# Batch by batch through two sweeps: reordering the first blocks of a fused attention and MoE kernel

## The chip, the cores and the metric

The kernel runs on one core of a Trainium2 chip. The metric is the device time of one execution in microseconds (us); the smaller, the better. Five engines work from queues of their own, each in the order in which the program was written: PE (TensorE: matmuls and transposes; its weight loads are listed as PEld), DVE (VectorE), ACT (ScalarE), POOL (GpSimd) and SP (SyncE), which issues DMA transfers. An engine whose next instruction has to wait holds back all that stands behind it.

## The reference

For 8 batches of 8 heads, 576 rows of 64 numbers, and a feature map phi of 32 columns:

```
a = softmax(phi, axis=2)                    # phi: batch, head, 576 rows, 32 columns
k_m = einsum('bhsm,bhsd->bhmd', a, k);  v_m = einsum('bhsm,bhsd->bhmd', a, v)
attn = softmax(q @ k_m.T / 8)               # 576 x 32
x = concat_heads(attn @ v_m)                # 4608 x 512
x = (h - tanh(h)) @ w_out,  h = x @ w_in    # 512 -> 2048 -> 512
out = elu(x @ w_in2) @ w_out2               # 512 -> 2048 -> 512
```

The first softmax runs along the axis of 576 rows, and its sums have 32 entries for each head. The inputs are float32 or float64 (the weights); products are formed from a high and a low part (hi, lo), three matmuls for each product.

## The kernel before

**Units.** A unit of attention is one batch and four heads; there are 16. `unit` (L108) is a generator: between two `yield`s it writes a few instructions. One call of `units.round()` (L253) advances every live unit by one such piece. A unit finds the column maxima of phi (`cmax`, DVE, L120), subtracts them (L135), takes the exponential `a` (ACT, L140), sums it over the rows (`asum`, DVE, L143), multiplies `a` with k and v on PE (`km`, L150; the sums' last step is L153), divides (L159 to L165), transposes, forms the scores (L195), takes the second softmax (L200 to L208) and stores its hi and lo parts in DRAM (`p_dram`, L222). Two Attention objects with buffers of their own, at0 and at1, take the units: 0 and 2 run in at0, all others in at1; units 0 and 1 start at rounds 0 and 1, units 2 and 3 at rounds 8 and 9, unit u from 4 on at round 22 + 7(u-4).

**Blocks.** Layer 1 works in 64 blocks, each one half of a batch (288 tokens, number n) in one of four sweeps `sw` (512 of the 2048 hidden columns). A block is two steps. A step computes `h_ps` (PE, L331, 12 matmuls) out of `p` and `vw`, then h - tanh(h) on ACT, POOL and DVE (`g_a` to `g_d`, L336 to L365), and beside it the output products `x_ps` (L376) of an earlier block, copied to `x2` tiles and stored (L391). The product v_m w_in (`vw`, L316) is formed in halves, four for each group of four blocks, in the fourth block of the group before. At L614 the blocks are listed: a group is a sweep and a pair of batches, so the first four blocks are two batches in sweep 0 and the next four are the same two batches in sweep 1.

**Weights.** `conv` (L524) loads 512 KB of float64 weights (`raw`), splits them on ACT, DVE and POOL (L48 to L60) and leaves hi and lo parts. `cv.round()` advances these generators; `need` calls it until a given part is there. Layer 2's weights go to DRAM the same way during layer 1. After block 63 layer 2 runs (L669), and the change doesn't touch it.

Of the kernel before, what the change touches and what calls it, by code (L numbers as in the profile page):

```python
# [8 lines left out]
F32 = mybir.dt.float32  # L9
# [53 lines left out]
class Attention:  # L63
# [5 lines left out]
    def __init__(self, tc, ctx, const, ins, vm, p_dram, side, psum):  # L69
        nc = tc.nc  # L70
        self.nc, self.ins, self.vm, self.p_dram = nc, ins, vm, p_dram
        self.ident, self.pmask, self.ones = const["ident"], const["pmask"], const["ones"]
        pool = lambda name, n: ctx.enter_context(
            tc.tile_pool(name=name + side, bufs=n, side=side, reuse_waits="tile"))
        self.wk = pool("at_wk", 1)
        self.sm = pool("at_sm", 2)
        self.sc_p = pool("at_sc", 2 if side == "left" else 1)
        self.ps = psum
        self.q_p = pool("at_q", 2)
        self.loaded = {}  # L80
# [4 lines left out]
        self.asum = fix.tile([128, 4, M], F32, name="asum")  # L85
        for t in (self.a, self.asum, self.kv):
            nc.gpsimd.memset(t[96:], 0.0)
        nc.gpsimd.memset(self.kT, 0.0)

    def load(self, u, what):  # L90
# [9 lines left out]
        elif what == "phi":  # L100
            t = self.wk.tile([96, 4, 6, M], F32, tag="phi", name="phi")
            nc.sync.dma_start(out=t, in_=view("phi", 0, 4))
        else:
            t = self.q_p.tile([96, 2, 6, D], F32, tag="q", name="q")
            nc.sync.dma_start(out=t, in_=view("q", 0 if what == "q0" else 2, 2))
        self.loaded[u, what] = t

    def unit(self, u, nxt, eng, first_p=None):  # L108
# [5 lines left out]
        kv, a, kT, asum = self.kv, self.a, self.kT, self.asum  # L114
# [5 lines left out]
        nc.vector.tensor_reduce(cmax, ph.rearrange("p h c m -> p h m c"), axis=AX.X, op=ALU.max)  # L120
# [22 lines left out]
        nc.vector.tensor_reduce(asum[:96], a[:96].rearrange("p c h m -> p h m c"), axis=AX.X, op=ALU.add)  # L143
        yield
# [12 lines left out]
        rm = sm.tile([128, 2, 1], F32, tag="rm", name="rm")  # L157
# [3 lines left out]
        nc.vector.tensor_scalar(rm[:, :, 0], self.pmask, rs, None, op0=ALU.mult)  # L161
# [3 lines left out]
        nc.vector.tensor_tensor(vbd, twice(1), rm.to_broadcast([128, 2, D]), op=ALU.mult)  # L165
        yield
        s = self.sc_p.tile([128, 18, M], F32, tag="s", name="s")
        for pr in range(2):
            qt = self.loaded.pop((u, f"q{pr}"))
            qT = wk.tile([128, 2, 3, 96], F32, tag="qT", name="qT")  # L170
            for h in range(2):
# [7 lines left out]
                yield  # L179
# [37 lines left out]
        yield  # L217
        for c, t in enumerate(first_p or ()):
# [64 lines left out]
class Moe1:  # L283


    def __init__(self, tc, ctx, const, p_dram, x2_dram):
# [7 lines left out]
        self.vw_p = pool("vw", 1)  # L294
        self.vw, self.p, self.g, self.x2, self.work, self.x2_pool = {}, {}, {}, {}, {}, {}
# [10 lines left out]
    def vw_half(self, vm, wi, pg, po, pars=(0, 1)):  # L306
        nc = self.nc
        if po == 0:
            for par in pars:
                self.vw[par, pg] = [self.vw_p.tile([128, 2, 256], F32R, tag=f"vw{pg % 2}_{par}{t}", name="vw")  # L310
# [180 lines left out]
def moe_kernel(tc, q, k, v, phi, w1, w2, w3, w4, out):  # L491
    nc = tc.nc
    with ExitStack() as top, tc.manual_schedule():
# [84 lines left out]
        def unit(u):  # L578
            if u % 4 == 0 and u:
                new_vm(u // 4)  # L580
            if u in (0, 2):
                yield from at0.unit(u, 2 if u == 0 else 2 * B, nc.vector if u == 0 else nc.gpsimd,
                                    first_p if u == 0 else None)
            else:
                yield from at1.unit(u, 3 if u == 1 else u + 1, nc.vector if u < 2 else nc.gpsimd,
                                    first_p if u == 1 else None)
# [7 lines left out]
        while 1 not in p_done:  # L594
            units.round()
# [19 lines left out]
        blocks = [(ss, bp, sub, j) for ss, bp, sub in groups for j in range(4)]  # L615
# [67 lines left out]
        for bi, (ss, bp, sub, j) in enumerate(blocks):  # L683
# [17 lines left out]
            vw_next = None  # L701
            if bi == 1:
                vw_next = (0, 0, (1,))
            elif j == 3 and nxt:
                vw_next = (nbp, 2 * nxt[0], (0, 1))
            if at0_open and 2 in p_done:
# [21 lines left out]
            for i in range(2):  # L728
# [92 lines left out]
```

## Time and profile before

| what | value |
|---|---|
| median of 3 runs | 1772.01 us (1768.45 to 1779.19) |
| the profiled execution's own time | 1771.73 us |
| its span, first to last instruction | 1770.0 us |
| PE busy | 1618.5 us, 91% of the span |
| DVE, ACT, POOL busy | 1225.3, 954.7, 766.3 us |
| chain that ended last | PE 70%, DMA 10%, DVE 7%, ACT 5% of the span |

A busy PE is no proof of a PE at its peak: at the lower of its two clocks the same matmul takes twice as long and is counted as busy all the same. The shares are means over stages with different limits, so the rows further down are taken by stage.

### The profile page before, as it was taken

The numbers are of one execution on the slowest core, as the hardware profiler recorded it, in microseconds if no ns is written. First come the engines' busy times: TensorE is split into PE (matmuls) and PEld (weight loads), VectorE is DVE, ScalarE is ACT, GpSimd is POOL, SyncE is SP. The second block draws the span as 40 slices with busy tenths as digits, with TensorE's granted clock in tenths as the row PEclk, the third lists the DMA queues.
The fourth block names the chain that finished last, engine by engine and source line by source line (L and its number), as shares of the span: only waits on it lengthen the run. The fifth ranks groups of instructions, "written<-read, shape, count | busy, mean of one in ns | idle before, by whom it ended". The sixth has DMA issues, their size and how long they took to land.

```text
span 1770.0 us, 30078 instructions
## 1 busy us (share of the span) xinstructions
PE 1618.5 (91%) x11496; PEld 1494.5 (84%) x11496; DVE 1225.3 (69%) x1805; ACT 954.7 (54%) x1713; POOL 766.3 (43%) x539
## 2 busy tenths in 40 slices
PE   4546887987998999999989999999999999999998
PEld 3446777877898999999989999999999999999997
DVE  5768876778899988888854555555555555555554
ACT  2445675766888888888864333333333333333332
POOL 2144554636676666666653222222222222222222
PEclk9668999999999999999999999999999999999999
DMA  9546557567566455666567521212222121111110
GB/s 226 157 121 181 146 158 201 169 191 221 187 225 195 160 177 212 217 215 223 189 191 291 195 61 60 60 60 60 60 60 59 54 58 56 57 60 57 58 36 25
DMA packets 140935, 238.40 MB, mean 135 GB/s; under 512 B 8184, under 2 KB 102392, under 8 KB 138744
## 3 DMA queue, kind: packets, MB, share of 16 engines
q1 hardware_dynamic: 140792, 236.49, 43.0%
q8 instruction: 91, 1.49, 0.4%
q14 instruction: 52, 0.43, 0.1%
HBM read 159.78 MB, written 75.50 MB: 133 GB/s over the span
## 4 chain that ended last, share of the span: by engine, by line
PE 70%; DMA 10%; DVE 7%; ACT 5%; issue 3%; POOL 2%; SPq 1%; DVEq 0%; POOLq 0%; ACTq 0%
PE h_ps L432 23%; PE o_ps L469 22%; PE x_ps L376 14%; PE h_ps L331 8%; DMA x_dram<-x 5%; DMA raw<-in_moe_w_in_dram 3%; PE vw_ps L316 2%; DVE s L356 1%; DVE vw L321 1%; DMA kv<-in_v_dram 1%; ACT t L342 1%; DMA xr<-x_dram 1%; DMA phi<-in_phi_dram 1%; ACT u L343 1%; ACT big L345 1%
## 5 line engine op out<-in xcount | busy, mean ns | idle before, releaser
L376 PE MATMUL x_ps<-g,w 128*128 128x288 f32 x3072 | 454.5, 301 | 30.4 <-DVE vw L321 9.6
L376 PEld LDWEIGHTS x_ps<-g,w 128*128 128x128 f32 x3072 | 427.2, 192 | 41.6 <-ACT x L383 11.0
L458 POOL TENSOR_TENSOR e<-hm,e 128x512 fp32r<-128x512 f32 x144 | 186.8, 1297 | 588.1 <-ACT e L457 435.4
L432 PEld LDWEIGHTS h_ps<-x,wi 128*128 128x128 f32 x3456 | 429.7, 190 | 11.7
L432 PE MATMUL h_ps<-x,wi 128*128 128x256 f32 x3456 | 433.2, 281 | 0.0
L469 PE MATMUL o_ps<-wo,e 128*128 128x512 f32 x1728 | 423.8, 394 | 0.7 <-POOL e L458 0.7
L469 PEld LDWEIGHTS o_ps<-wo,e 128*128 128x128 f32 x1728 | 314.8, 188 | 65.0 <-POOL e L458 1.1
L443 ACT ACTIVATE t_ps<-hm 128x512 f32<-128x512 f32 x144 | 86.7, 602 | 515.1 <-DVE hm L442 515.1
L350 POOL TENSOR_TENSOR v<-t,u 128x576 f32<-128x576 f32 x128 | 183.9, 1436 | 230.8 <-ACT u L343 208.4
L331 PE MATMUL h_ps<-p,vw 128*128 128x288 f32 x1536 | 241.8, 309 | 17.8 <-DVE s L357 6.1
L331 PEld LDWEIGHTS h_ps<-p,vw 128*128 128x128 f32 x1536 | 222.9, 199 | 20.9 <-issue 12.7
L364 POOL TENSOR_TENSOR g<-s,g 128x576 fp32r<-128x576 f32 x128 | 203.2, 1588 | 83.9 <-ACT g L363 81.3
L449 DVE SCALAR_TENSOR_TENSOR hm<-hm,t_ps 128x512 f32<-128x512 f32 x144 | 99.1, 688 | 200.6 <-ACT hm L444 200.6
L442 DVE TENSOR_SCALAR hm<-h_ps 128x512 f32<-128x512 f32 x144 | 99.6, 692 | 139.9 <-PE h_ps L432 139.9
L351 DVE TENSOR_TENSOR h_ps<-h_ps,t 128x576 f32<-128x576 f32 x128 | 97.9, 765 | 56.8 <-ACT u L343 55.6
L342 ACT ACTIVATE t<-h_ps 128x576 f32<-128x576 f32 x128 | 83.2, 650 | 82.2 <-PE h_ps L331 39.6
L356 DVE SCALAR_TENSOR_TENSOR s<-s,v 128x576 f32<-128x576 f32 x128 | 121.5, 949 | 1.8 <-POOL v L350 1.8
L321 DVE TENSOR_TENSOR vw<-vw_ps,vw 64x512 fp32r<-64x512 f32 x128 | 88.1, 688 | 40.4 <-ACT vw L319 38.4
L357 DVE COPY_PREDICATED s<-big,h_ps 128x576 f32<-128x576 uint32 x128 | 106.3, 831 | 11.3 <-DVE s L356 0.5
L345 ACT ACTIVATE big<-u,bias 128x576 f32<-128x576 f32 x128 | 97.5, 762 | 13.5 <-DVE s L357 13.5
L451 DVE TENSOR_TENSOR hm<-hm,h_ps 128x512 f32<-128x512 f32 x144 | 98.9, 687 | 5.0
L450 DVE SCALAR_TENSOR_TENSOR hm<-hm,t_ps 128x512 f32<-128x512 f32 x144 | 98.9, 687 | 4.9
(86 smaller groups left out, 1764.6 us busy)
## 6 DMA issues: line engine op xcount, KB each, us to landing
x_dram<-x SPq DMA_DIRECT2D x128, 288.0 KB
xr<-x_dram SPq DMA_DIRECT2D x72, 512.0 KB
p<-p_dram SPq DMA_DIRECT2D x62, 576.0 KB
raw<-in_moe_w_in_dram SPq DMA_DIRECT2D x32, 512.0 KB
raw<-in_moe_w_out_dram SPq DMA_DIRECT2D x32, 512.0 KB
w_dram<-wst SPq DMA_DIRECT2D x32, 512.0 KB
kv<-in_k_dram SPq DMA_DIRECT2D x16, 576.0 KB
kv<-in_v_dram SPq DMA_DIRECT2D x16, 576.0 KB
```

The costliest lines, as they stand in the source:

```text
L321: nc.vector.tensor_tensor(lo, src, r32(hi), op=ALU.subtract)
L331: nc.tensor.matmul(ps[:, j, :NB], lhsT=vw[a][:, kc, 128 * j:128 * j + 128], rhs=p[:, kc, b, :], start=(k == 0), stop=(k == 5))
L342: nc.scalar.activation(t, w[0], ACTF.Tanh)
L345: nc.scalar.activation(big, u, ACTF.Relu, bias=bias[:, 1:2])
L350: nc.gpsimd.tensor_tensor(v, t, u, op=ALU.mult)
L356: nc.vector.scalar_tensor_tensor(s, s, G_B, v, op0=ALU.add, op1=ALU.mult)
L357: nc.vector.copy_predicated(s, big.bitcast(U32), d)
L364: nc.gpsimd.tensor_tensor(g[:, 1], s, r32(g[:, 0]), op=ALU.subtract)
L376: nc.tensor.matmul(ps, lhsT=wo[pg][:, a, j, 128 * dm:128 * dm + 128], rhs=g[:, b, j, :], start=(k == 0), stop=(k == 11))
L432: nc.tensor.matmul(ps[:, j], lhsT=w3[:, a, kc, 128 * j:128 * j + 128], rhs=x[:, b, kc, :], start=(k == 0), stop=(k == 11))
L458: nc.gpsimd.tensor_tensor(e[:, 1], hm, r32(e[:, 0]), op=ALU.subtract)
L469: nc.tensor.matmul(self.acc[n][tg], lhsT=e[:, a, j, 128 * tg:128 * tg + 128], rhs=w4[:, b, j, :], start=(pg == 0 and j == 0 and i == 0), s ...
```

## The change

Layer 1's first eight blocks are put in another order: the first batch in sweep 0 and then in sweep 1, then the second batch. at0 takes unit 0 alone; at1 takes all others in a row, unit u from 2 on at round 8 + 7(u-2). The `vw` of these blocks are formed for one batch at a time, with a free slot given by `vw_first`. The sums of `a` are formed on PE out of `a` itself (six matmuls) in place of `asum` on DVE and four matmuls; the column maxima come from three elementwise steps in place of one reduction; `rm` goes and its factor is folded into `vbd`. phi is issued on ACT's queue from unit 2 on; kv and q loads are written one piece later. From block 26 on, the four halves of `vw` are spread over the last two blocks of a group, one for each step. The pool of `x2` tiles grows from 3 to 4, that of the `s` tiles (`gw`) shrinks from 3 to 2.

```diff
@@ Attention.load, unit
-            nc.sync.dma_start(out=t, in_=view("phi", 0, 4))
+            (nc.sync if u < 2 else nc.scalar).dma_start(out=t, in_=view("phi", 0, 4))
-        nc.vector.tensor_reduce(cmax, ph.rearrange("p h c m -> p h m c"), axis=AX.X, op=ALU.max)
+        nc.vector.tensor_tensor(top, ph[:, :, 0:3], ph[:, :, 3:6], op=ALU.max)
+        nc.vector.tensor_tensor(cmax, top[:, :, 0], top[:, :, 1], op=ALU.max)
+        nc.vector.tensor_tensor(cmax, cmax, top[:, :, 2], op=ALU.max)
-        nc.vector.tensor_reduce(asum[:96], a[:96].rearrange("p c h m -> p h m c"), axis=AX.X, op=ALU.add)
-        yield
-        for h in range(4):
-            nc.tensor.matmul(km[32 * h:32 * h + 32, 2 * D:], lhsT=asum[:, h], rhs=self.ones[:, :2],
-                             start=True, stop=True)
-        self.load(nxt, "kv")
+        for c in range(6):
+            nc.tensor.matmul(km[:, 2 * D:], lhsT=a[:, c].rearrange("p h m -> p (h m)"), rhs=self.ones[:, :2],
+                             start=(c == 0), stop=(c == 5))
-        nc.vector.tensor_scalar(rm[:, :, 0], self.pmask, rs, None, op0=ALU.mult)
-        nc.vector.tensor_tensor(vbd, twice(1), rm.to_broadcast([128, 2, D]), op=ALU.mult)
+        for j in range(2):
+            nc.vector.tensor_scalar(vbd[:, j], kmv[:, 1], rs, self.pmask[:, j:j + 1], op0=ALU.mult, op1=ALU.mult)
+        yield
+        self.load(nxt, "kv")
@@ Moe1.__init__
-        self.x_p = pool("x2", 3)
+        self.x_p = pool("x2", 4)
-        self.gw, self.gw1 = pool("gw", 3), pool("gw1", 1)
+        self.gw, self.gw1 = pool("gw", 2), pool("gw1", 1)
@@ moe_kernel, units and blocks
-            if u in (0, 2):
-                yield from at0.unit(u, 2 if u == 0 else 2 * B, nc.vector if u == 0 else nc.gpsimd,
-                                    first_p if u == 0 else None)
+            if u == 0:
+                yield from at0.unit(u, 2 * B, nc.vector, first_p)
-        for u, t in ((0, 0), (1, 1), (2, 8), (3, 9)):
-            units.at(t, unit(u))
-        for u in range(4, 2 * B):
-            units.at(22 + 7 * (u - 4), unit(u))
+        for u in range(2 * B):
+            units.at(u if u < 2 else 8 + 7 * (u - 2), unit(u))
-        blocks = [(ss, bp, sub, j) for ss, bp, sub in groups for j in range(4)]
+        blocks = [(0, 0, sub, j) for j0 in (0, 2) for sub in range(2) for j in (j0, j0 + 1)]
+        blocks += [(ss, bp, sub, j) for ss, bp, sub in groups[2:] for j in range(4)]
+        vw_first = {1: (0, 2, (0,), 1), 3: (0, 0, (1,), 0), 5: (0, 2, (1,), 1)}
+            if j >= 2 and bi >= 26:
+                if bi // 4 + 1 < len(groups):
+                    nss, nbp, nsub = groups[bi // 4 + 1]
+                    vw_spread = (nbp, 2 * (2 * nss + nsub) + j - 2)
+            elif bi in vw_first:
+                vw_next = vw_first[bi]
-            if at0_open and 2 in p_done:
+            if at0_open:
...
+                if vw_spread:
+                    vbp, vpg = vw_spread
+                    need("i", vpg)
+                    m1.vw_half(vm[vbp], wi[vpg], vpg, i)
```

Where the rows now stand is told by the program's order on each engine. On DVE, while the first two batches' attention runs and before the first block. Before (`asum`, `rm` and two units' divisions):

```order
L143 TENSOR_REDUCE asum<-a 96x128
L50 TENSOR_SCALAR cv_m<-cv_m 128x512
L51 TENSOR_SCALAR cv_m<-cv_m 128x512
L200 TENSOR_REDUCE smax<-s 128x18
L201 TENSOR_TENSOR s<-s,smax 128x576
L159 TENSOR_SCALAR rs<-km 128x1
L160 RECIPROCAL rs<-rs 128x1
L161 TENSOR_SCALAR rm<-pmask,rs 128x2
L163 TENSOR_SCALAR kk<-km,rs 128x128
L165 TENSOR_TENSOR vbd<-km,rm 128x128
L143 TENSOR_REDUCE asum<-a 96x128
```

The same place in the changed program:

```order
L199 TENSOR_REDUCE smax<-s 128x18
L200 TENSOR_TENSOR s<-s,smax 128x576
L157 TENSOR_SCALAR rs<-km 128x1
L158 RECIPROCAL rs<-rs 128x1
L160 TENSOR_SCALAR kk<-km,rs 128x128
L163 TENSOR_SCALAR vbd<-km,rs,pmask 128x64 x2
L50 TENSOR_SCALAR cv_m<-cv_m 128x512
```

The reductions of `a` and `rm` are gone, and unit 3's division no longer stands ahead of the first block; it follows in block 0.

On PE, around the second block's first step. Before (w_376 is part 0 of w_in, here with the second batch; w_616 and w_752 are parts of w_out):

```order
L331 MATMUL h_ps<-p,vw 128x288 x12
L150 MATMUL km<-kv,a 32x128 x24
L153 MATMUL km<-ones,asum 32x2 x4
L316 MATMUL vw_ps<-w_376,vm 128x256 x6
L376 MATMUL x_ps<-g,w_616 128x288 x6
L376 MATMUL x_ps<-g,w_752 128x288 x6
L174 MATMUL pq<-ident,q 128x96 x3
L316 MATMUL vw_ps<-w_376,vm 128x256 x6
L331 MATMUL h_ps<-p,vw 128x288 x12
```

The same place in the changed program (w_862 is part 2 of w_in, which stood two blocks later):

```order
L335 MATMUL h_ps<-p,vw 128x288 x12
L181 MATMUL kT_ps<-ident,kk 128x128
L182 MATMUL kT_ps<-ident,vbd 128x128
L320 MATMUL vw_ps<-w_862,vm 128x256 x6
L380 MATMUL x_ps<-g,w_576 128x288 x6
L380 MATMUL x_ps<-g,w_770 128x288 x6
L194 MATMUL sc<-qT,kT 64x288 x2
L127 MATMUL mT<-ident,cmax 128x96
L320 MATMUL vw_ps<-w_862,vm 128x256 x6
L335 MATMUL h_ps<-p,vw 128x288 x12
```

Parts 2 and 3 of w_in are now due in block 1, and not in block 3; w_out's parts 2 and 3 move up likewise. From the tenth block on, both programs hold the same number of units and conversions at the same block.

On PE, at a change of groups in the second half of layer 1. Before:

```order
L316 MATMUL vw_ps<-w_5814,vm 128x256 x6
L331 MATMUL h_ps<-p,vw 128x288 x12
L376 MATMUL x_ps<-g,w_6927 128x288 x6
L376 MATMUL x_ps<-g,w_7216 128x288 x6
L316 MATMUL vw_ps<-w_5972,vm 128x256 x6
L376 MATMUL x_ps<-g,w_6927 128x288 x6
L376 MATMUL x_ps<-g,w_7216 128x288 x6
L316 MATMUL vw_ps<-w_5972,vm 128x256 x6
L331 MATMUL h_ps<-p,vw 128x288 x12
```

The changed program:

```order
L320 MATMUL vw_ps<-w_5889,vm 128x256 x6
L335 MATMUL h_ps<-p,vw 128x288 x12
L380 MATMUL x_ps<-g,w_7002 128x288 x6
L380 MATMUL x_ps<-g,w_7306 128x288 x6
L380 MATMUL x_ps<-g,w_7002 128x288 x6
L380 MATMUL x_ps<-g,w_7306 128x288 x6
L320 MATMUL vw_ps<-w_6058,vm 128x256 x6
L335 MATMUL h_ps<-p,vw 128x288 x12
```

A step held two halves of `vw` with a product `x_ps` between them, and now holds one, right ahead of the next step.

## Rows read from the trace of the kernel before

**Rows 1.** Stages: us, busy PE, PEld, DVE, ACT, POOL; clock, DMA share, GB/s.

```profile
0.00:77.00 77.00, 35.70 (x332) 24.31 (x332) 54.34 (x105) 25.01 (x55) 18.84 (x22) 0.88 0.90 215
77.00:177.00 100.00, 62.47 (x424) 53.50 (x425) 72.50 (x107) 51.83 (x97) 42.64 (x30) 0.76 0.50 138
177.00:260.00 83.00, 70.96 (x638) 65.05 (x638) 67.07 (x104) 59.47 (x118) 45.54 (x32) 0.97 0.54 158
260.00:490.00 230.00, 195.81 (x1663) 179.35 (x1662) 173.75 (x271) 160.13 (x315) 125.86 (x86) 0.95 0.62 189
490.00:600.00 110.00, 102.26 (x747) 100.63 (x746) 102.72 (x152) 93.96 (x164) 73.86 (x53) 0.97 0.60 201
600.00:893.00 293.00, 286.24 (x2143) 283.58 (x2143) 259.02 (x384) 252.56 (x440) 202.58 (x140) 1.00 0.58 201
893.00:946.00 53.00, 46.05 (x317) 45.64 (x316) 30.52 (x42) 31.10 (x52) 28.56 (x19) 0.90 0.77 231
946.00:1770.00 824.00, 819.01 (x5245) 742.50 (x5244) 465.43 (x645) 280.64 (x475) 228.43 (x162) 1.00 0.22 71
```

**Rows 2.** Timeline of PE: start, us, instructions; first steps of blocks 0, 4, 9.

```profile
77.00 1.30 PE L331 MATMUL h_ps<-p,vw 128*128 128x288 f32 x4 [3.44 <-DMA p<-phl]
...
177.11 1.16 PE L331 MATMUL h_ps<-p,vw 128*128 128x288 f32 x4
...
259.54 1.86 PE L331 MATMUL h_ps<-p,vw 128*128 128x288 f32 x12
```

**Rows 3.** Stage view, the stretch from 30 to 70 us.

```profile
30.00:70.00 40.00, 20.21 (x179) 12.20 (x180) 36.33 (x65) 15.84 (x37) 10.41 (x7) 0.82 0.82 200
```

**Rows 4.** Waits from 77 to 177 us: total, times, longest.

```profile
ACT cv_m L48 <- DMA raw<-in_moe_w_in_dram: 12.3, 3, 8.2
...
PE h_ps L331 <- DMA p<-p_dram: 3.8, 1, 3.8
```

**Rows 5.** Waits from 260 to 490 us.

```profile
ACT x L383 <- DMA x_dram<-x: 28.3, 9, 5.8
```

**Rows 6.** Chain that ended last, one group of four blocks.

```profile
637.33 1.61 PE h_ps L331 x12
...
679.30 0.71 PE vw_ps L316 x6
680.01 1.61 PE h_ps L331 x12
```

**Rows 7.** Timeline of PE at a change of groups.

```profile
677.47 1.83 PE L376 MATMUL x_ps<-g,w 128*128 128x288 f32 x12 [0.91 <-DVE vw L321]
...
679.85 1.77 PE L331 MATMUL h_ps<-p,vw 128*128 128x288 f32 x12
...
684.65 1.77 PE L331 MATMUL h_ps<-p,vw 128*128 128x288 f32 x12
```

**Rows 8.** Timeline of DVE at the end of layer 1.

```profile
928.82 0.46 DVE L385 COPY x<-x_ps 128x288 f32<-128x288 f32 x1 [7.49 <-DMA x_dram<-x]
```

**Rows 9.** Groups of DVE's instructions up to 260 us: busy us, mean ns.

```profile
L120 DVE TENSOR_REDUCE cmax<-phi 96x128 f32<-96x768 f32 x10 | 15.5, 1547 | 6.1 <-DMA phi<-in_phi_dram 6.1
L143 DVE TENSOR_REDUCE asum<-a 96x128 f32<-96x768 f32 x9 | 13.6, 1506 | 1.9 <-ACT a L140 1.9
...
L161 DVE TENSOR_SCALAR rm<-pmask,rs 128x2 f32<-128x2 f32 x9 | 6.4, 710 | 0.3
```

**Rows 10.** Line 201: shortest, median, longest ns; first and last start.

```profile
L201 DVE TENSOR_TENSOR s<-s,smax x16: 757/759/1877, 46.1 to 477.3; 128x576 f32<-128x576 f32 x16
```

**Rows 11.** Timeline of SP: start and us of an issue.

```profile
120.58 4.31 SPq L530 DMA_DIRECT2D raw<-in_moe_w_in_dram  x1
...
142.05 0.32 SPq L102 DMA_DIRECT2D phi<-in_phi_dram  x1
```

**Rows 12.** Timeline of all engines within a group of four blocks.

```profile
648.49 1.76 POOL L364 TENSOR_TENSOR g<-s,g 128x576 fp32r<-128x576 f32 x1 [1.42 <-ACT g L363]
...
649.85 0.78 ACT L344 ACTIVATE s<-u,bias 128x576 f32<-128x576 f32 x1
```

More of the change, by code (lines that the diff above doesn't have):

```diff
@@ L84, in __init__ @@
         self.kT = fix.tile([128, 4, 2, M], F32, name="kT")
-        self.asum = fix.tile([128, 4, M], F32, name="asum")
-        for t in (self.a, self.asum, self.kv):
+        for t in (self.a, self.kv):
             nc.gpsimd.memset(t[96:], 0.0)
@@ L113, in unit @@
         ident = self.ident
-        kv, a, kT, asum = self.kv, self.a, self.kT, self.asum
+        kv, a, kT = self.kv, self.a, self.kT
         ps_tile = lambda shape, name: self.ps.tile(shape, F32, tag="m", name=name)
@@ L309, in vw_half @@
             for par in pars:
-                self.vw[par, pg] = [self.vw_p.tile([128, 2, 256], F32R, tag=f"vw{pg % 2}_{par}{t}", name="vw")
+                at = par if slot is None else slot
+                pool = self.vw2_p if self.vw2_p and par and pg // 2 % 2 else self.vw_p
+                self.vw[par, pg] = [pool.tile([128, 2, 256], F32R, tag=f"vw{pg % 2}_{at}{t}", name="vw")
                                     for t in range(2)]
@@ L580, in unit @@
                 new_vm(u // 4)
-            if u in (0, 2):
-                yield from at0.unit(u, 2 if u == 0 else 2 * B, nc.vector if u == 0 else nc.gpsimd,
-                                    first_p if u == 0 else None)
-            else:
-                yield from at1.unit(u, 3 if u == 1 else u + 1, nc.vector if u < 2 else nc.gpsimd,
-                                    first_p if u == 1 else None)
+            if u == 0:
+                yield from at0.unit(u, 2 * B, nc.vector, first_p)
+            else:
+                yield from at1.unit(u, u + 1, nc.vector if u < 2 else nc.gpsimd, first_p if u == 1 else None)
         first_p = [m1.new_p(0, n) for n in range(2)]
         units = Staged()
-        for u, t in ((0, 0), (1, 1), (2, 8), (3, 9)):
-            units.at(t, unit(u))
-        for u in range(4, 2 * B):
-            units.at(22 + 7 * (u - 4), unit(u))
+        for u in range(2 * B):
+            units.at(u if u < 2 else 8 + 7 * (u - 2), unit(u))
         while 1 not in p_done:
+            if units.rounds >= 7:
+                cv.half()
             units.round()
@@ L746, in moe_kernel @@
                 if vw_next:
-                    vbp, vpg, pars = vw_next
+                    vbp, vpg, pars, slot = vw_next
                     need("i", vpg + i)
-                    while ss == 0 and not all(u in vm_done for u in range(4 * vbp + 4)):
+                    while ss == 0 and not all(u in vm_done for u in range(4 * vbp + 2 * len(pars) + 2 * pars[0])):
                         units.round()
-                    m1.vw_half(vm[vbp], wi[vpg + i], vpg + i, 0, pars)
+                    m1.vw_half(vm[vbp], wi[vpg + i], vpg + i, 0, pars, slot)
                 if soon and bi > 60:
@@ L761, in moe_kernel @@
                 if vw_next:
-                    m1.vw_half(vm[vbp], wi[vpg + i], vpg + i, 1, pars)
+                    m1.vw_half(vm[vbp], wi[vpg + i], vpg + i, 1, pars, slot)
+                if vw_spread:
+                    vbp, vpg = vw_spread
+                    need("i", vpg)
+                    m1.vw_half(vm[vbp], wi[vpg], vpg, i)
                 pend.append((n, pg))
-            if ss == 0 and sub == 0 and j == 1:
+            if ss == 0 and (bi == 5 or bi >= 8 and sub == 0 and j == 1):
                 save_vm(bp)
```

18 lines of the change are left out of this document (10 added, 8 removed).

## The prediction

> **What bounds the kernel now.** I read the stages first [rows 1]. From 600 to 893 us PE works 286 of 293 us at full clock, and from 946 us on 819 of 824: there PE is the limit. Ahead of 600 us it is not. PE is idle 41 us of the first 77, 38 of the next 100, 12 of 83, 34 of 230 and 8 of 110; from 893 to 946 another 7. Up to 177 us the granted clock is below full as well (0.88, 0.76), so even the busy time there is stretched. Whatever this change can win lies in these 140 us of idle time and in that clock.
>
> Next I looked for what each stage waits for. Before the first block DVE is full: 36.33 us of the 40 between 30 and 70 [rows 3]; the first block starts at 77.00 [rows 2]. Block 4 starts at 177.11 and block 9 at 259.54, so the first four blocks take 25 us each, the next five 16.5 [rows 2]. In the first four, ACT waits 12.3 us in three pieces for weights that have only just been asked for, and PE 3.8 us for a reloaded `p` [rows 4]. From 260 to 490 us ACT waits nine times, 28.3 us in all, to copy an output product into an `x2` tile whose store has not landed [rows 5], and PE stands behind it.
>
> In the PE-bound stage a group of four blocks takes 680.01 - 637.33 = 42.68 us [rows 6]. A step without `vw` takes 684.65 - 679.85 = 4.80 us [rows 7] and half of `vw` 0.71 us [rows 6]; eight steps and four halves are 41.24. The other 1.44 us is a stall at the change of groups: PE waits there for DVE's part of a `vw` product [rows 7], since four PSUM results fall in one step and three buffers take them in turn.
>
> **The change part by part, and the sum.** All is reckoned against the profiled execution, 1771.7 us; the median of the runs, 1772.0, is the same.
>
> *Before the first block.* DVE loses four `asum` (1.51 us each) and four `rm` (0.71 each) [rows 9], 8.9 us, in a stretch where it is full. Two of the four sums stand before 30 us, where DVE had room; against that, unit 3's division and one conversion's first half leave the stretch too. I take -9: first block at 68 us. Bounds: 0, if the units' own chain of some twenty pieces or the loads take over (the DMA share is 0.90 in this stage [rows 1]); -13, if all that leaves counts.
>
> *Blocks 0 to 8.* The first four blocks no longer need units 2 and 3, but need w_in's parts 2 and 3 two blocks earlier. At the pace of the next five blocks they take 4 x 16.5 = 66 us; I keep the waits for weights and `p` whole (12.3 + 3.8), which gives 82 and not 100: -18. Four more halves of `vw` are formed, 4 x 0.71 = 2.8. The units' rounds that left the first blocks come back among blocks 2 to 8: I add 5 us, under a third of a block. Together -10. Bounds: -30 (PE idles 50 us in these two stages), and +10 (first rival).
>
> *Blocks 9 to 22, 260 to 490 us.* A fourth `x2` tile gives a store one more step to land. The longest of the nine waits is 5.8 us [rows 5], and a step lasts about 8 us here (16.5 a block), so most of the waits should go. Other transfers and chains are close behind; I take half of 28.3, -14. DVE loses 2.2 us for each of some twelve units, 26 us, but is full only 174 of 230 us; a sixth of it, -4. Together -18, between 0 and -34 (all PE idle time).
>
> *Column maxima.* The reduction (1.55 us) [rows 9] becomes three two-input steps of 384, 128 and 128 columns. A two-input step of 576 columns takes 0.76 in the middle and 1.88 at the worst [rows 10]: so 0.51 and twice about 0.3 if nothing holds them, 1.1 in all; and 1.12 us more for each if each is held, 4.5. The median row is not held: I count the swap at nothing.
>
> *Loads.* phi is issued from ACT 14 times. An issue of phi took 0.32 us on SP [rows 11], 4.5 us in all, beside ACT's spare time (160 busy of 230): nothing. If the queue holds an issue as long as that of a weight load at 120.58, 4.31 us [rows 11], it is 60 us of ACT time, in the stage whose bound is already open to 0 above. The later kv loads spare SP a wait for `km`; what they are next to meet is `km` of the next unit, seven rounds later: nothing. The sums on PE cost 2 short matmuls more a unit: nothing beside 196 us of PE work.
>
> *Spread `vw`.* Nine changes of groups are spread. Seven lie between 600 and 893 us: 7 x 1.44 = -10, between -10 and 0. Two lie between 490 and 600, where PE idles 8 us in all: I take -5, between -8 and 0.
>
> *End of layer 1.* DVE waits 7.49 us for an `x2` slot at 928.82 [rows 8], and PE idles 7 us in this stage; a fourth slot was stored one step earlier. -6, between -7 and 0. Layer 2 keeps its order: 0.
>
> Sum: -9 - 10 - 18 - 5 - 10 - 6 = -58, so 1713.7: **1714 us**.
>
> **Rivals.** *The early gain is lost to the weights.* Eight conversions of 512 KB move up by two blocks, right behind the first block, and ACT stands still at each one that has not landed (8.2 us was the longest wait [rows 4]). For it: units 2 and 3 now run beside them on DVE, 72 of 100 us busy here. Against: the DMA share is 0.50 in this stage, so the loads may start into idle queues. Price: blocks 0 to 8 cost +10 in place of -10: 1734. Chance 0.12.
>
> *Slower: two `s` tiles.* With two tiles ACT may write `s` (L344) only when POOL's subtraction of the step before last (L364) is done. In the row at 648.49 that subtraction lasts until 650.25, while ACT wrote at 649.85 [rows 12]: 0.40 us late even now. If POOL falls behind in every step, the 128 steps take on its pace. It decides from 0.6 us a step (76 us, more than the 58 won and the 18 of one per cent); at that pace the time is 1790. Against: such a lag is absorbed as long as ACT has time to spare, 253 busy of 293 us, and PE sets the step. Chance 0.04.
>
> *The stores do not land sooner.* If the queues and not the number of tiles set the pace (189 GB/s in that stage, 231 at the end), the gain at the `x2` waits stays out, and the early blocks go as in the first rival: -9 + 10 - 4 - 0 - 10 - 3 = -16, 1756. For: two of the terms taken here rest on the same stores. Against: a longest wait of 5.8 us, shorter than the step gained. Chance 0.07.
>
> *The column maxima are held in every unit.* Each of the three steps waits for POOL as long as the longest of the sixteen did [rows 10]: 4.5 us in place of 1.55, 16 x 2.9 = 47 us of DVE time, of which a sixth shows, as above: +8, so 1722. Against: the median of the row, 0.76, lies at its minimum. Chance 0.07. The Trainium skill, "GPSIMD Engine Reference", "1. Specifications", says that GpSimd's SBUF interfaces are shared with VectorE, with contention for VectorE instructions that have two SBUF inputs, which speaks against this swap: by that rule alone the sum would be 1722, by the row's median 1714.
>
> *More than forecast.* With fewer waits the clock of 0.76 in the second stage rises too, and the blocks there win 25, those after 260 us 28: 1689. Chance 0.10.
>
> The forecast itself has 0.60, with a range of its own from 1695 to 1735.
>
> **The numbers.** About 1% (18 us) is what a measurement of this kernel can tell from no change. Below 1754 lie the forecast, the first rival and the last two, 0.89, less a little for their tails: faster 0.88. Within 1%: the stores' case, 0.08. Slower 0.04. The range reaches from the best case to just short of the stores' case: 1688 to 1750.
>
> **What would show each step.** The first `h_ps` at 65 to 71 us. Block 4's first step at 150 to 165 us, block 9's at 232 to 248. ACT's waits for weights in the second stage not above some 20 us. ACT's waits for `x_dram` between blocks 9 and 22 under 8 us. A group in the PE-bound stage at 41.2 to 41.5 us and no wait of `x_ps` for `vw`. The wait of 7.49 us at the end gone or under 3. I am wrong if the tenth block starts later than 255 us, if ACT's L344 gets waits on POOL of more than 0.3 us a step, or if the waits for `x_dram` come back under another transfer's name.

## The result, and the profile after

The changed kernel takes 1757.31 us (median of 5 runs, 1752.37 to 1762.41) against 1773.53 us before (five runs as well), a ratio of 0.990 [0.987, 0.993]: 16 us faster, where 58 were forecast and 22 were the least that the range allowed. The profiled execution took 1762.41 us, span 1760.6; the longest of the five.

Five of the stages after, with the columns of [rows 1]:

```profile
0.00:77.00 77.00, 45.48 (x358) 33.92 (x359) 51.91 (x112) 26.62 (x56) 21.01 (x22) 0.75 0.84 215
77.00:177.00 100.00, 66.09 (x488) 59.34 (x488) 74.49 (x123) 56.60 (x109) 49.75 (x35) 0.79 0.49 140
177.00:260.00 83.00, 69.55 (x608) 62.45 (x608) 55.86 (x96) 53.69 (x109) 37.51 (x27) 0.96 0.53 155
260.00:490.00 230.00, 204.40 (x1713) 187.64 (x1712) 165.03 (x277) 160.21 (x314) 125.60 (x87) 0.95 0.64 194
...
600.00:893.00 293.00, 290.21 (x2183) 288.56 (x2182) 263.87 (x390) 257.65 (x448) 209.88 (x140) 1.00 0.60 203
```

From 260 to 490 us PE is 9 us busier and DVE 9 us less busy than before: work went from DVE to PE. The first steps of blocks 0, 4 and 9 on PE, which answer to [rows 2]:

```profile
62.77 2.79 PE L335 MATMUL h_ps<-p,vw 128*128 128x288 f32 x12
...
165.66 1.78 PE L335 MATMUL h_ps<-p,vw 128*128 128x288 f32 x12
...
265.04 1.86 PE L335 MATMUL h_ps<-p,vw 128*128 128x288 f32 x12
```

Block 0 starts 14 us earlier, block 4 only 11, block 9 is 5.5 us late. All of the early gain is gone by the tenth block. What PE waits for from 77 to 177 us (total, times, longest), beside [rows 4]:

```profile
PE vw_ps L320 <- ACT w L58: 14.0, 1, 14.0
...
PE vw_ps L320 <- POOL w L60: 7.4, 3, 4.2
```

ACT no longer waits for raw parts of w_in; now PE waits 21 us for the parts of w_in that ACT and POOL have yet to form. Waits from 260 to 490 us, beside [rows 5]:

```profile
DVE top L120 <- DMA phi<-in_phi_dram: 11.6, 2, 6.3
...
DVE rs L157 <- PE km L153: 8.3, 6, 3.6
```

The waits for `x_dram` are gone from this stretch, as forecast. In their place DVE waits for phi and for the sums. DVE's and PE's groups within the units, whole run (busy, mean ns | idle before), beside [rows 9]:

```profile
L120 DVE TENSOR_TENSOR top<-phi 96x384 f32<-96x384 f32 x16 | 12.0, 750 | 17.8 <-DMA phi<-in_phi_dram 17.8
...
L122 DVE TENSOR_TENSOR cmax<-cmax,top 96x128 f32<-96x128 f32 x16 | 8.9, 559 | 0.5
L121 DVE TENSOR_TENSOR cmax<-top 96x128 f32<-96x128 f32 x16 | 7.0, 437 | 0.6
...
L157 DVE TENSOR_SCALAR rs<-km 128x1 f32<-128x1 f32 x16 | 2.5, 155 | 25.8 <-PE km L153 25.8
```

```profile
L153 PE MATMUL km<-ones,a 128*128 128x2 f32 x192 | 26.4, 265 | 0.0
```

Last, ACT's first tanh of five groups of four blocks, beside [rows 6]:

```profile
634.94 0.65 ACT L346 ACTIVATE t<-h_ps 128x576 f32<-128x576 f32 x1 [0.16 <-issue]
...
676.22 0.65 ACT L346 ACTIVATE t<-h_ps 128x576 f32<-128x576 f32 x1 [0.15 <-issue]
...
758.78 0.65 ACT L346 ACTIVATE t<-h_ps 128x576 f32<-128x576 f32 x1 [0.15 <-issue]
802.32 0.65 ACT L346 ACTIVATE t<-h_ps 128x576 f32<-128x576 f32 x1
846.37 0.65 ACT L346 ACTIVATE t<-h_ps 128x576 f32<-128x576 f32 x1
```

A group takes 41.28 us, as forecast; but two late ones take 43.5 and 44.1. There ACT waits for a store of layer 2's weights; in the first of them, from 758 to 802 us:

```profile
ACT wst L58 <- DMA w_dram<-wst: 3.7, 3, 1.9
```

### The profile page after: what moved, and what is told of

It is laid out like the page before. It is cut to its first block, busy times and chain, and to the rows that moved or that the text cites. A ratio compares the mean times of both kernels' runs of the same rounds, so it can differ in the third digit from the quotient of the medians.

```text
span 1760.6 us, 30412 instructions
## 1 busy us (share of the span) xinstructions
PE 1632.2 (93%) x11584; PEld 1508.8 (86%) x11584; DVE 1202.7 (68%) x1821; ACT 954.6 (54%) x1713; POOL 768.1 (44%) x537
## 4 chain that ended last, share of the span: by engine, by line
PE 72%; DMA 8%; DVE 8%; ACT 6%; issue 4%; POOL 2%; SPq 0%; ACTq 0%; DVEq 0%; POOLq 0%
PE h_ps L436 23%; PE o_ps L473 23%; PE x_ps L380 13%; PE h_ps L335 7%; DMA p<-p_dram 3%; DMA phi<-in_phi_dram 2%; PE vw_ps L320 2%; DMA w_dram<-wst 2%; PE km L150 1%; PE km L153 1%; ACT t L346 1%; DVE s L360 1%; POOL g L368 1%; DVE vw L325 1%; ACT big L349 1%
## 5 line engine op out<-in xcount | busy, mean ns | idle before, releaser
L380 PE MATMUL x_ps<-g,w 128*128 128x288 f32 x3072 | 445.5, 299 | 15.5 <-ACT x L387 12.7
L335 PE MATMUL h_ps<-p,vw 128*128 128x288 f32 x1536 | 239.6, 307 | 11.4 <-DVE s L361 6.6
L453 DVE SCALAR_TENSOR_TENSOR hm<-hm,t_ps 128x512 f32<-128x512 f32 x144 | 99.0, 688 | 200.3 <-ACT hm L448 200.3
L348 ACT ACTIVATE s<-u,bias 128x576 f32<-128x576 f32 x128 | 99.6, 778 | 21.0 <-POOL g L368 11.1
L320 PE MATMUL vw_ps<-w,vm 128*128 128x256 f32 x432 | 72.2, 306 | 35.7 <-ACT w L58 14.0
```

The costliest lines, as they stand in the source:

```text
L320: nc.tensor.matmul(ps[:, kc], lhsT=vm[:, a, p, :], rhs=wi[:, b, p, :], start=(i == 0), stop=(i == 2))
L335: nc.tensor.matmul(ps[:, j, :NB], lhsT=vw[a][:, kc, 128 * j:128 * j + 128], rhs=p[:, kc, b, :], start=(k == 0), stop=(k == 5))
L380: nc.tensor.matmul(ps, lhsT=wo[pg][:, a, j, 128 * dm:128 * dm + 128], rhs=g[:, b, j, :], start=(k == 0), stop=(k == 11))
```

## The experiments

Each ratio is to the kernel before, on the same chip. Where two variants are compared, their difference is that of their medians. In five sets of runs the kernel before had medians from 1773.5 to 1776.2 us, so that up to 3 us between two variants measured apart says nothing. A forced round is a call of `units.round()` that a block makes because the `p` or the v_m that it needs is not there yet; nothing of a block stands between its pieces. My theory, once the profile was read: **the new order only moves the units' and the weights' work, so that forced rounds take back what it wins, and the sums on PE cost time besides.** Rival: the order wins as forecast, and the edits inside the units eat it. In the end the rival came nearer.

### What the edits inside the units cost

**e2_sums_dve.**

> The changed kernel with the sums of a as before (one reduction on DVE, four small matmuls). Theory (each unit's six matmuls of 128 columns of weights cost PE 1.2 us that DVE then waits for): PE busy falls by about 20 us, the stretch 260 to 490 us is 3 to 8 us shorter in spite of 1.5 us of DVE work per unit, the first block 3 to 6 us later; in all -6 to +2 us against 1757. Rival (DVE is what the units wait for, the matmuls cost nothing): nothing won after the first block, 6 to 15 us slower than 1757.

```diff
+        nc.vector.tensor_reduce(asum[:96], a[:96].rearrange("p c h m -> p h m c"), axis=AX.X, op=ALU.add)
+        yield
...
-        for c in range(6):
-            nc.tensor.matmul(km[:, 2 * D:], lhsT=a[:, c]..., rhs=self.ones[:, :2], start=(c == 0), stop=(c == 5))
+        for h in range(4):
+            nc.tensor.matmul(km[32 * h:32 * h + 32, 2 * D:], lhsT=asum[:, h], rhs=self.ones[:, :2], ...)
```

1748.52 us, 0.985 [0.983, 0.987]: 8.8 us faster than the change, more than either theory said. Its groups:

```profile
L146 DVE TENSOR_REDUCE asum<-a 96x128 f32<-96x768 f32 x16 | 24.4, 1523 | 2.2 <-ACT a L143 2.2
...
L160 DVE TENSOR_SCALAR rs<-km 128x1 f32<-128x1 f32 x16 | 2.4, 148 | 9.5 <-PE km L156 9.4
```

```profile
L156 PE MATMUL km<-ones,asum 128*32 128x2 f32 x128 | 3.7, 175 | 1.7 <-DVE asum L146 1.7
```

The reduction costs DVE 24.4 us; but PE's share falls from 26.4 to 3.7 us and DVE's wait for it from 25.8 to 9.5. The first block came 9 us later, and nothing of that was left in the second. The edit also gives each unit back one piece, a `yield` behind the reduction; e14 shows below what one piece is worth.

**e7_phi_on_sp.**

> The kernel of e2_sums_dve with every load of phi issued on SP as before. Theory (the queue that issues phi matters little; phi comes late because its buffer comes free late): waits of the maxima for phi as in e2, some 12 us, time within 4 us of 1748.5. Rival (on SP the load stands behind stores of x2 and p that wait): waits of DVE for phi above 25 us, 5 to 12 us slower.

```diff
-            (nc.sync if u < 2 else nc.scalar).dma_start(out=t, in_=view("phi", 0, 4))
+            nc.sync.dma_start(out=t, in_=view("phi", 0, 4))
```

1737.74 us, 0.978 [0.977, 0.980]: 10.8 us faster than e2. Both theories missed; phi on ACT's queue costs, and the rival had the sign wrong.

**e8_max_reduction.**

> The kernel of e2_sums_dve with the column maxima as one reduction, as before. Theory (three steps of 0.7, 0.35 and 0.45 us cost about what one of 1.55 us did): the maxima take 24 to 25 us of DVE in all, time within 4 us of 1748.5. Rival (three two-input steps hold POOL up and are held by it): 5 to 10 us faster than e2.

```diff
-        nc.vector.tensor_tensor(top, ph[:, :, 0:3], ph[:, :, 3:6], op=ALU.max)
-        nc.vector.tensor_tensor(cmax, top[:, :, 0], top[:, :, 1], op=ALU.max)
-        nc.vector.tensor_tensor(cmax, cmax, top[:, :, 2], op=ALU.max)
+        nc.vector.tensor_reduce(cmax, ph.rearrange("p h c m -> p h m c"), axis=AX.X, op=ALU.max)
```

1745.02 us, 0.983 [0.981, 0.985]: 3.5 us faster than e2, within the intervals.

**e16_only_phi_on_sp.**

> The changed kernel with phi issued on SP and nothing else undone. Theory (phi late on ACT's queue costs its own 8 to 11 us, beside what the sums cost): 1746 to 1750. Rival (phi's lateness hides behind DVE's waits for the sums): within 4 us of 1757.

The edit of e7 on the changed kernel itself. 1745.01 us, 0.982 [0.980, 0.985]: 12.3 us faster than the change. So phi's cost doesn't hide behind the sums.

**e9_units_as_before.**

> The changed kernel with the three edits inside the units undone together: the sums of a on DVE, the maxima as one reduction, phi issued on SP; order, x2 and s tiles, spread and later loads as changed. Theory (each of the three cost time, 9, 11 and 3 us by the runs so far, and they add): 1731 to 1737. Rival (they share one wait, that of the units for their phi): 1737 to 1745.

The edits of e2, e7 and e8 together. **1734.10 us, 0.977 [0.975, 0.979]**: 23.2 us faster than the change; singly they gave 8.8, 10.8 and 3.5, 23.1 in all. They add. Against e8 phi alone is worth 10.9 us, the third such pair. A load of phi in the change, and one in e9 (start, us, instruction):

```profile
211.00 0.41 ACTq L101 DMA_DIRECT2D phi<-in_phi_dram  x1
...
223.62 0.55 DVE L120 TENSOR_TENSOR top<-phi 96x384 f32<-96x384 f32 x1 [4.41 <-DMA phi<-in_phi_dram]
```

```profile
250.94 0.31 SPq L102 DMA_DIRECT2D phi<-in_phi_dram  x1
...
254.74 1.55 DVE L120 TENSOR_REDUCE cmax<-phi 96x128 f32<-96x768 f32 x1
```

The issue is as short on either queue (0.41, 0.31 us). But the first was used 12.6 us after its issue, when DVE had waited 4.4 us for it, and the second after 3.8 us without a wait. This pair is an extreme one. Over the fourteen loads from unit 2 on, the median from issue to the last packet is 6.3 us in the change and 3.4 in e16, 6.1 in e2 and 3.0 in e7, 5.6 in e8 and 3.2 in e9. On DVE all that stands behind the maxima in the program's order waits with them. DVE's wait for phi over the whole run (the last column) in e2, e7, e8, e9 and e16:

```profile
L121 DVE TENSOR_TENSOR top<-phi 96x384 f32<-96x384 f32 x16 | 11.1, 693 | 11.9 <-DMA phi<-in_phi_dram 11.9
L121 DVE TENSOR_TENSOR top<-phi 96x384 f32<-96x384 f32 x16 | 11.9, 744 | 7.5 <-DMA phi<-in_phi_dram 7.5
L120 DVE TENSOR_REDUCE cmax<-phi 96x128 f32<-96x768 f32 x16 | 24.7, 1545 | 10.4 <-DMA phi<-in_phi_dram 10.4
L120 DVE TENSOR_REDUCE cmax<-phi 96x128 f32<-96x768 f32 x16 | 24.8, 1549 | 8.7 <-DMA phi<-in_phi_dram 8.7
L120 DVE TENSOR_TENSOR top<-phi 96x384 f32<-96x384 f32 x16 | 12.0, 752 | 1.8 <-DMA phi<-in_phi_dram 1.8
```

From the change to e16 this wait falls by 16.0 us, but from e2 to e7 by 4.4 and from e8 to e9 by 1.7, for much the same gain. So it is shown that the move costs 11 to 12 us and that phi lands later from ACT's queue; it is not shown that DVE's wait for phi is all that leads from the one to the other.

### What the order is worth

**e1_old_order.**

> The changed kernel with the blocks, the at0/at1 share of the units and their starts as before; all else as changed. Theory (the new order only moves the units' work and the weights' work: what it wins up to block 3 it gives back in the rounds of units that are still forced ahead of blocks 8 and 10): block 9 starts within 5 us of the changed kernel's, and the time is within 8 us of its 1757. Rival (the order itself wins the 10 to 18 us of the forecast, and the sums on PE and phi on ACT's queue eat it): block 9 10 to 18 us later than in the changed kernel, 1767 to 1775.

```diff
-        blocks = [(0, 0, sub, j) for j0 in (0, 2) for sub in range(2) for j in (j0, j0 + 1)]
-        blocks += [(ss, bp, sub, j) for ss, bp, sub in groups[2:] for j in range(4)]
+        blocks = [(ss, bp, sub, j) for ss, bp, sub in groups for j in range(4)]
...
-            units.at(u if u < 2 else 8 + 7 * (u - 2), unit(u))
+            units.at(u if u < 2 else 6 + u if u < 4 else 22 + 7 * (u - 4), unit(u))
```

1761.52 us, 0.992 [0.990, 0.994]: 4.2 us slower than the change, not told apart from it. With the units as changed the order is worth next to nothing, as the theory had it: block 4's first tanh comes 11.4 us later than in the change, block 24's 2.7. Block 9, though, was 6 us late, where the theory said 5 at most.

**e10_order_undone_too.**

> The kernel of e9 with the order of blocks and units as before as well. Theory (the order wins what the first block wins and little more, since the units' forced rounds and the weights pulled ahead eat the rest): 5 to 11 us slower than e9, block 10 within 12 us of e9's. Rival (with the units cheap again, the order wins the 20 us and more that the forecast gave it): 18 us or more slower than e9.

e9 with e1's edit. 1748.93 us, 0.985 [0.983, 0.987]: 14.8 us slower than e9, between the two theories. So the order does win, once the units are as before: the theory's first half falls there, and holds for the changed units alone. Where, the first tanh of some blocks tells (us; each column one profiled execution):

| block | before | after | e2 | e9 | e10 | e5 | e11 | e12 |
|---|---|---|---|---|---|---|---|---|
| 0 | 80.3 | 65.6 | 74.3 | 75.8 | 80.2 | 74.2 | 74.0 | 76.5 |
| 1 | 106.4 | 89.8 | 88.3 | 91.1 | 104.9 | 88.5 | 88.1 | 93.5 |
| 4 | 179.7 | 167.5 | 164.4 | 165.6 | 181.4 | 165.6 | 163.5 | 170.6 |
| 7 | 226.3 | 215.8 | 213.0 | 210.3 | 228.4 | 214.1 | 208.5 | 222.8 |
| 9 | 263.1 | 266.9 | 258.7 | 255.3 | 270.9 | 244.3 | 238.5 | 262.6 |
| 16 | 385.0 | 388.2 | 376.2 | 367.9 | 381.7 | 357.7 | 350.0 | 382.3 |
| 24 | 504.0 | 502.1 | 488.1 | 479.6 | 493.7 | 493.7 | 489.9 | 484.2 |
| 36 | 639.0 | 634.9 | 622.0 | 612.5 | 626.5 | 643.3 | 633.3 | 620.8 |
| 60 | 895.1 | 887.6 | 869.7 | 860.2 | 878.6 | 900.5 | 888.0 | 871.8 |

Between e10 and e9, 4.4 us lie at block 0, 15.8 at block 4, 18.1 at block 7, and 14 to 16 from block 9 up to block 36. The order wins its time up to block 4 and keeps it.

**e6_no_w23_wait** (the first use of w_in's parts 2 and 3 takes parts 0 and 1).

> The kernel of e2_sums_dve, but the first products of the first batch with parts 2 and 3 of w_in (formed in block 1) take parts 0 and 1 in their place, so nothing in blocks 0 to 3 waits for the conversion of parts 2 and 3; every other use of them stays. Theory (the conversions pulled ahead hold the first four blocks, 14 us of PE's waits for parts of w_in there): block 4 starts 5 to 12 us earlier than e2's 164.4 us, and by block 9 less than half of it is left, since the forced rounds there wait for the units. Rival (the units' own work holds blocks 0 to 3): block 4 within 3 us of e2's.

```diff
-                    need("i", vpg + i)
+                    src = vpg + i if bi != 1 else i
+                    need("i", src)
...
-                    m1.vw_half(vm[vbp], wi[vpg + i], vpg + i, 0, pars, slot)
+                    m1.vw_half(vm[vbp], wi[src], vpg + i, 0, pars, slot)
```

1753.09 us, 0.988 [0.986, 0.991]. Block 2 comes 9.9 us earlier than in e2, and then block 4 10.3 us later, so both theories miss. From 136 to 176 us:

```profile
PE x_ps L383 <- ACT w L58: 14.0, 3, 7.2
...
ACT cv_m L48 <- DMA raw<-in_moe_w_out_dram: 12.9, 2, 8.2
```

The wait moved on to the parts of w_out, whose conversions follow in the same row. The edit has a side effect: `need` also drives the conversions, and without its calls in block 1 the first two loads for w_out are issued at 106.85 and 112.47 us, in e2 at 98.84 and 102.49. So the one part of w_in is not all that bounds blocks 0 to 3. That the whole row of weights does, which the order pulls ahead, fits these waits, but is not parted from the later loads.

### Forced rounds, or the units' work?

**e5_pair2_by_batch.**

> The kernel of e2_sums_dve (the change with the sums of a on DVE) with the second pair of batches also worked batch by batch in both sweeps, so that block 7 needs the v_m of units 4 and 5 only and block 9 no attention of units 6 and 7 (units 12 to 15 start six rounds later). Theory (the early gain is given back where rounds of the units are forced: two in block 7, four ahead of block 9; steps 15 to 18 take 35 us there): the stall at step 18 goes, block 11 starts 4 to 10 us earlier than in e2, some of it is kept, 1740 to 1747. Rival (the units' work itself, not its place, is the bound; it comes back in other steps): block 16 and the time within 3 us of e2's 1748.5, or later by the 2.8 us of the four further halves of vw.

```diff
-        blocks = [(0, 0, sub, j) for j0 in (0, 2) for sub in range(2) for j in (j0, j0 + 1)]
+        blocks = [(0, bp, sub, j) for bp in range(2) for j0 in (0, 2) for sub in range(2) for j in (j0, j0 + 1)]
...
-            units.at(u if u < 2 else 8 + 7 * (u - 2), unit(u))
+            units.at(u if u < 2 else 8 + 7 * (u - 2) + 6 * (u > 11), unit(u))
...
```

1770.16 us, 0.997 [0.995, 0.998]: block 16 comes 18.5 us earlier than in e2, as the theory had it, and block 36 21 us later. At block 26 PE waits for the `p` of units that came too late:

```profile
523.82 3.22 PE L338 MATMUL h_ps<-p,vw 128*128 128x288 f32 x12 [8.85 <-DMA p<-p_dram]
```

**e11_pair2_no_late_end.**

> The kernel of e9 with the second pair of batches worked batch by batch too, as in e5, but units 12 to 15 started at rounds 84, 90, 96 and 102, so that the last starts 3 rounds late and not 6. Theory (e5 won 14 to 18 us by block 16 where no rounds are forced, and lost it where units 14 and 15 came too late for blocks 24 to 27): the early part is kept, the late loss falls to less than 20 us; 1728 to 1745. Rival (the late loss is the units' work itself, met by the conversions): as slow as e5 against its base, 1750 or more.

e5's order on e9, with `84 + 6 * (u - 12)` as the start of units 12 to 15. 1763.48 us, 0.993 [0.991, 0.995]. Block 16 is 17.9 us earlier than in e9, block 36 20.8 later: nearly the same loss, with the units only 3 rounds late and PE's longest wait for `p` at 3.8 us in place of 8.9. The rival holds.

**e12_units_every_6.**

> The kernel of e9 with units 2 to 15 started every 6 rounds, not every 7, so that units 6 and 7 are through about five rounds earlier and next to no round is forced in block 7 and ahead of block 10. Theory (a forced round stalls PE, since nothing of a block stands between its pieces): steps 15 to 18 shrink by 8 us or more, some of it is kept, 4 to 10 us faster than e9. Rival (it is the units' work that counts, wherever it stands): within 3 us of e9.

`8 + 6 * (u - 2)` in e9. 1746.37 us, 0.983 [0.981, 0.985]: 12.3 us slower. Blocks 7 to 9 shrink from 45.0 to 39.8 us, but block 7 itself comes 12.5 us later. In e5, e11 and e12 alike the forced rounds are not a stall that one can take away: the units' work shows wherever it is put, and packed closer it shows more. The theory falls in its second half too.

**e14_store_as_before.**

> The kernel of e9 without the added piece ahead of the store of p, so each unit from the fifth on is through one round earlier. Theory (a round more or less moves work and takes none away): within 4 us of e9's 1734. Rival (it is one more forced round in block 7 and ahead of block 10): 4 to 8 us faster.

```diff
-        if u >= 4:
-            yield
         for c, t in enumerate(first_p or ()):
```

The change added this piece to the units from unit 4 on; the part on the change does not list it. 1739.06 us, 0.979 [0.977, 0.981]: 5.0 us slower than e9, a little more than the theory's 4, but not told apart from it, though block 9's first step starts at 246.28 us and not at 253.38.

**e13_loads_as_before.**

> The kernel of e9 with the loads of kv and q written where they were before, one piece earlier. Theory (as forecast, the later place of the loads is worth nothing): within 4 us of e9's 1734. Rival (earlier loads make SP wait for the matmuls that read the old tile, and the loads and stores behind them come late): 5 to 10 us slower. Other rival (the later place makes kv late): 5 to 10 us faster.

```diff
-        yield
-        self.load(nxt, "kv")
+        self.load(nxt, "kv")
...
+        yield
```

(and q likewise.) 1739.80 us, 0.980 [0.977, 0.982]: 5.7 us slower than e9, but not told apart from it; the rival's 5 to 10 us are not ruled out.

### The tiles and the spread

**e3_x3_s3.**

> The changed kernel with three x2 tiles and three s tiles, as before. Theory (two s tiles hold ACT where POOL lags; four x2 tiles spare the waits for stores): the groups of four blocks after 760 us, now 43.5 and 44.1 us, go back to 41.2 to 41.5, 5 us won; the waits of ACT for x_dram between 260 and 490 us and of DVE at the end come back, 5 to 15 us lost; time 1757 to 1767. Rival (POOL's lag there has another cause): the two groups stay above 43 us.

```diff
-        self.x_p = pool("x2", 4)
+        self.x_p = pool("x2", 3)
-        self.gw, self.gw1 = pool("gw", 2), pool("gw1", 1)
+        self.gw, self.gw1 = pool("gw", 3), pool("gw1", 1)
```

1766.38 us, 0.995 [0.993, 0.997]: 9.1 us slower. The waits from 260 to 490 us come back, though only a quarter of those of [rows 5]:

```profile
ACT x L387 <- DMA x_dram<-x: 7.6, 3, 4.0
```

Of the late groups one still takes 43.5 us with three `s` tiles, and in e1, e2 and e9 all take 41.3 with two. Two `s` tiles by themselves do not bring the late groups.

**e15_x3_s3_again.**

> The kernel of e9 with three x2 and three s tiles, as before. Theory (the fourth x2 tile spares waits for stores, as e3 showed by 9 us): 1739 to 1746. Rival (with the units faster the stores land in time anyway): within 3 us of 1734.

The same edit on e9: 1743.65 us, 0.982 [0.980, 0.984], 9.5 us slower than e9. By the first tanh of the blocks, 2.8 us of it lie ahead of block 9 and 5.8 between blocks 60 and 63. From block 9 to block 24 it takes 224.5 us, and e9 224.3. Waits from 855 to 925 us, in e15 and then in e9:

```profile
DVE x L389 <- DMA x_dram<-x: 8.1, 2, 7.5
...
DVE x L389 <- DMA x_dram<-x: 2.1, 1, 2.1
```

**e4_no_spread.**

> The changed kernel with the four halves of vw of a group back in its fourth block from block 26 on. Theory (each change of groups costs 1.44 us of stall, and the spread form takes it away, but sends POOL into a lag in two groups): groups at 42.7 us in the stage bound by PE, the lag after 760 us gone or smaller, time 1757 to 1764. Rival (the lag is not due to the spread): the two late groups 44 to 45.5 us, time 1766 to 1770.

```diff
-            if j >= 2 and bi >= 26:
+            if j >= 2 and bi >= 99:
```

1766.23 us, 0.994 [0.993, 0.996]: 8.9 us slower. A group takes 42.77 us again:

```profile
637.81 0.65 ACT L346 ACTIVATE t<-h_ps 128x576 f32<-128x576 f32 x1 [0.46 <-issue]
...
680.58 0.65 ACT L346 ACTIVATE t<-h_ps 128x576 f32<-128x576 f32 x1 [0.46 <-issue]
```

All its late groups take 42.7, with the spread away: at first sight the lag is the spread's, but e1, e2 and e9 have the spread and no lag.

## Why the prediction was wrong

**The step that failed first: "The sums on PE cost 2 short matmuls more a unit: nothing beside 196 us of PE work."** I counted matmuls and columns of output, and not the columns of weights. They take 26.4 us of PE, 1.65 a unit, where the old ones with 32 columns of weights took 3.7; PE is busy 21 us longer than in e2 (1632.2 against 1611.0), and DVE stood behind it 16 us longer. Worth 8.8 us (e2). Late units' sums, in the change beside a step's twelve matmuls of 288 columns, and before:

```profile
442.16 1.50 PE L153 MATMUL km<-ones,a 128*128 128x2 f32 x12
...
444.31 1.76 PE L335 MATMUL h_ps<-p,vw 128*128 128x288 f32 x12
```

```profile
449.33 0.22 PE L153 MATMUL km<-ones,asum 128*32 128x2 f32 x8
```

The six matmuls stand as twelve records, and two columns of output in place of 288 save 0.26 us of 1.76. The old four matmuls also write four strips of `km` of their own, while the new six add up in one place; how much of the difference is the weights' width and how much the strips, no run tells apart. The Trainium skill, "TensorE: Matmul & The Clock Gate", "LDWEIGHTS (loading the stationary operand)", says that loading weights takes time by their columns, P / 1.2 ns for P of them; an estimate from that page is 107 ns for 128, times twelve loads a unit 1.28 us. The trace agrees in part: 26.4 us over 192 records are 0.138 us for each; a load's own row lasts 192 ns (median) with 128 columns and 110 ns with 32, both longer than by the page, but 82 ns apart where the page has 80.

**"An issue of phi ... beside ACT's spare time: nothing."** The issue was as cheap as forecast; the landing was not. I bounded the price by ACT's time, and never asked when phi lands. Worth 10.8 to 12.3 us in three pairs, of which DVE's wait for phi covers the whole in one pair only. The Trainium skill, "DMA: Bandwidth & Descriptors", "Issuing engines are not separate DMA queues", says that a second issuing engine saves only the time to issue. The trace agrees that nothing is gained; that a load can land later from there (a median of 6.3 us against 3.4) stands in these runs alone. Why it does is open.

**"I count the swap [of the maxima] at nothing."** 27.9 us in place of 24.9, and 3.5 and 3.6 us in two pairs whose intervals overlap: next to right. The first step's mean is 0.75 us where its shortest is 0.54, so some of the steps are held, but far from all, as the rival with 47 us had it.

**Blocks 0 to 8, "together -10".** In the changed kernel they lost 18.5 us (80.3 to 263.1 before, 65.6 to 266.9 after), and block 9's first step came at 265.04 us, past the 255 that I had set as a sign of being wrong. With the units as before, the order came to the forecast's sum: e10 to e9, it wins 11.2 us between blocks 0 and 9. But there two misses cancel: 11.3 us are won up to block 4, where the forecast has about 15, and nothing is given back in the next five, where it has 5. What ate it in the changed kernel were the edits above, and a piece that I gave no term at all, the one added ahead of the store of `p`: e10, with the order of before, is 7.8 us later than before at block 9, and without that piece e14 is 7.1 us earlier there than e9 (one execution each). By the end that is not told from nothing. The first rival, with the weights, is right on the place: PE waits there for parts of w_in, and for w_out's when those are taken away (e6); but it costs near the 16.1 us that I had kept in the sum (21.4 in the change, 13.6 in e9), not 20 us more.

**"Before the first block ... -9".** It came to -14.7, past the bound of -13, and was worth nothing: e2 and e9 start 9 and 10 us later and are level in block 1, where PE's wait for a part of w_in is 14.0 us in the change and 5.7 in e9. The early start is only a longer wait. In e9, from 77 to 177 us:

```profile
PE vw_ps L320 <- ACT w L58: 5.7, 1, 5.7
```

**Blocks 9 to 22, "-18".** In the changed kernel -5.7 (from block 9 to block 24), in e9 -16.6. That the second is near the forecast is luck, for neither of its two terms shows there. The fourth tile, with the third `s` tile gone, is worth 9 us over the whole run (e3, e15), but e15 without it takes as long as e9 from block 9 to 24. With three tiles 7.6 (e3) and 11.5 us (e15) of the 28.3 us of waits come back, and they do not set the pace of the stretch. The -4 rests on sums that e9 has on DVE again. Nor was DVE spared 2.2 us for each unit: its busy time fell by 22.6 us in all, 1.4 a unit, since the maxima take 3 us more and `vbd` takes two steps of 0.34 us where it took one of 0.28. What wins the 16.6 us is open: e10, with the order of before, wins 18.1 there, and no run undoes the fold of `rm` by itself.

**Spread.** The size of a group was right to 0.1 us, 1.49 us a change. Against the 15 forecast the medians with e4 show 8.9. By the blocks' first tanh, the two changes between 490 and 600 us gave 2.4 against e4 (blocks 24 to 32, 94.1 and 91.7 us) and less than 1 against the kernel before, not 5: DVE is busy 103 of 110 us there, which speaks for DVE and not PE's stall as the bound. The other seven gave 10.3, and the two late groups of the profiled execution took 5.0 back.

**End, -6.** It was -2.1 in the changed kernel (from block 60 to the second step of block 63) and -3.3 in e9: the wait for an `x2` tile fell but did not go, and DVE waits longer for layer 2's first loads. From 893 to 946 us, in the kernel before and then in the changed one:

```profile
DVE x L385 <- DMA x_dram<-x: 8.1, 2, 7.5
DVE xr L414 <- DMA xr<-x_dram: 4.8, 2, 4.5
...
DVE xr L418 <- DMA xr<-x_dram: 8.6, 2, 8.0
DVE x L389 <- DMA x_dram<-x: 3.3, 1, 3.3
```

e9 is the forecast's kernel without its three failed zeros: 1734 us, at the upper end of the forecast's own range of 1695 to 1735. That it lies inside is no proof of the sum: it also gives up the time on DVE that the sums on PE were to spare, and the terms above do not all hold in it. It beats both kernels. What is left to 1714 are, by the table and block 63, the first block (4.5), blocks 0 to 8 (6.7), blocks 9 to 22 (1.4), the spread between 490 and 600 (4) and the end (3). The slower rival, two `s` tiles, showed only faintly: ahead of `s` ACT waits for POOL 11.1 us in the changed kernel, 6.5 in e9 and not at all before, 0.09 us a step at most, where the rival needed 0.6.

Open: why stores of layer 2's weights land late in some executions (two groups of this profile, also in e7, e8, e10, e12, e13 and e16, and not in e1, e2, e4, e6, e9, e11 and e14, in the same part of the program); why phi lands later from ACT's queue, and what beside DVE's wait makes it dear; what wins the time in blocks 9 to 22.

## What to carry to other kernels

Whatever is counted at nothing needs its own row: here three zeros cost 23 us and hid a gain of 15. A total that comes out right is no proof of its terms: undo each by itself. Price a matmul by its weights' columns as well as by its output's, and a load by when it lands, not by its issue. And work that is moved out of a stall can come back where it is put (e5, e11, e12); before a reordering is credited, find the next thing that the block will wait for.

## What the runs showed of the hardware

A matmul of two columns with 128 columns of weights took 0.138 us of PE for each record, nearly five times the 0.029 us (3.7 over 128) with 32 columns in four strips: moving a sum to PE "for free" was dearer there than 1.52 us on DVE. A 288 KB load issued on ACT's queue had its last packet after 6.3 us (median of fourteen), one on SP's busy queue in e16 after 3.4. And a first block that starts 10 us earlier was worth nothing by the second.
